# Choosing the most loaded expert two attention units earlier, and fetching its weights three units earlier

## The chip, the cores and the metric

The kernel runs on one core of a Trainium2 chip. The metric is device time in microseconds of one execution. The engines are TensorE (PE), VectorE (DVE), ScalarE (ACT), GpSimd (POOL) and SyncE (SP); SP computes nothing here and issues most DMA transfers, in program order, while POOL issues the indirect ones.

## The reference

Three stages follow one another on 1536 tokens of width 512:

```python
# attention: 2 batches, 8 heads, 768 positions, 64 wide
scores_l = scale * q @ k.T, kept where abs(i - j) < 16      # local window
scores_s = scale * q @ k_sum.T + log(32)                    # 24 block summaries: max of k, mean of v
x = softmax([scores_l, scores_s]) @ [v, v_sum]              # 1536 x 512
# mixture of 8 experts: tokens with x @ w_skip > 0 take their best expert, the others pass
e = argmax(xc @ w_gate); gate = softmax(xc @ w_gate)[e]
out[do] = xc + gate * (relu(xc @ w1[e]) @ w2[e])            # w1: 512 x 1024, w2: 1024 x 512 per expert
# feed-forward, 512 -> 2048 -> 512, with a piecewise quadratic g
out = g(x @ w_in) @ w_out
```

## The kernel before

Attention is cut into 24 **units**; unit i handles one 128-token tile and half of the heads, so that tile t is finished by units 2t and 2t+1 (the first six units go through their three tiles twice). Two units share a pair of V blocks. The units are software-pipelined: in the loop step of unit i, PE transposes the probabilities of unit i+1 (`stage_t`, tile `pt`), makes the scores of unit i+3 (`stage_s`, tile `s`), multiplies unit i's probabilities by V (`stage_pv`, tile `xo`), and between them prepares the q and k of the second batch (`prep`, tiles `tpk` and `pb`, up to unit 9). The order of the program in this stage is written by hand: `at(i, f, ...)` appends a function to the list of unit i, and the list is emitted behind unit i's `stage_pv`, in the order of the `at` calls. Every engine runs its own instructions in that order.

V is loaded by `load_v(b, j)` in blocks of 64 tokens, j = 0 to 11 for each batch, into six buffers `vw` that are used in turn. In the text **V1.j** is block j of the second batch; for j below 6 a small load from `vs_d` with the block summaries follows it (`put_vs`). Unit 12 reads V1.0 and V1.1, unit 14 reads V1.2 and V1.3, unit 16 reads V1.4 and V1.5, unit 18 reads V1.6 and V1.7, and so on. A buffer becomes free when the units that read its old block are done, so V1.2 and V1.3 wait for unit 9, V1.4 and V1.5 for unit 11, V1.6 and V1.7 for unit 13.

While attention runs, the tokens of finished tiles are routed: `r1` and `r2` make their expert scores, `r3` the one-hot choice and the running counts `run[t]` (a chain of small DVE instructions), `r4` each token's place, and POOL scatters the place lists and the rows to DRAM. Two experts' weights are wanted during attention already. The first is **the most loaded expert among the first three tiles**: `top` lets PE sum the counts (`count(3)`, a matmul with `run[3]`, tile `cnt`), and nine DVE instructions make an index of it in `placei`; `top_reg` loads that index into an SP register. `fetch(0, c)` for c = 0 to 3 then brings that expert's weights, 1 MB each, into the four `b8` buffers (in the text **W0 to W3**; line 129), and `split_hi` on ACT and `split_lo` on DVE (line 145) cut them into a high and a low part from unit 15 on, a half megabyte per unit. After attention, expert 0 is applied to its block of 128 tokens, then the other experts and the feed-forward follow.

All loads named here, V blocks and fetches alike, go through SP's one queue; a load that waits on SP holds back those behind it.

Of the kernel before, what the change touches and what calls it, by code (L numbers as in the profile page):

```python
# [40 lines left out]
def tile_net(ctx, tc, q, k, v, w_skip, w_gate, w1, w2, w_in, w_out, out):  # L41
# [243 lines left out]
    def attention(actx):  # L285
# [444 lines left out]
        def at(i, f, *a):  # L730
            todo[i].append(lambda: f(*a))
# [28 lines left out]
            at(c + 2, store_vs, c)  # L760
        rest = [(1, n // 4, n % 4) for n in range(16)]

        at(10, top)
        at(11, top_reg)
        at(16, early)
        at(17, early_places)
        at(18, early_regs)
# [3 lines left out]
        at(21, fetch, 1, 1)  # L771
        at(22, fetch, 1, 2)
        for c in range(4):
            at(12 + c, fetch, 0, c)

        pieces = [(0, c, i) for c in range(4) for i in range(4)]
        for n, x in enumerate(pieces):
# [544 lines left out]
    with ExitStack() as actx:  # L1322
        with tc.manual_schedule():
            attention(actx)
# [38 lines left out]
```

## Time and profile before

| | us |
|---|---|
| median of 3 runs | 550.04 |
| lowest, highest | 548.15, 554.98 |
| profiled execution, its own time | 547.05 |
| span in that profile, first to last instruction | 545.3 |

The profiled execution is one run of the same program, 3 us under the median of the others, and 1.75 us of it lie outside the span. PE is busy for 91% of the span, DVE for 65%, ACT for 52%. The page cuts the span into 40 slices of 13.6 us; attention fills about the first ten.

### The profile page before, as it was taken

To read this page: it belongs to the slowest core of one execution; us is meant where nothing else is said; L and a number is where in the kernel's file an instruction comes from. 1 tells how busy PE (TensorE), PEld (TensorE's weight loads), DVE (VectorE), ACT (ScalarE), POOL (GpSimd) and SP (SyncE) were. 2 spreads that over 40 slices of the span, in tenths; PEclk is the share of its full clock that TensorE was granted. 3 is DMA by queue.
4 is the path that set the end of the run, shared out by engine and by line. 5 is a ranking of instruction groups with operands and counts; after the bars stand their busy time and mean duration, and the time that the engine had idled before them with its cause. 6 is when DMAs were issued, how large, how long until landed. Compare 5 with 4: busy or idle time off the path is not lost.

```text
span 545.3 us, 7782 instructions
## 1 busy us (share of the span) xinstructions
PE 494.0 (91%) x2742; PEld 402.5 (74%) x2742; DVE 355.5 (65%) x714; ACT 285.7 (52%) x512; POOL 108.5 (20%) x159
## 2 busy tenths in 40 slices
PE   7777979688989999986899999999999999999990
PEld 4666868577678888854678887888888888888880
DVE  6667776769688978899999998443334443333340
ACT  6475545653457777682587776542334333333330
POOL 8406431503534131332000000020000020000002
PEclk8999999875989999998899999999999999999996
DMA  8997417996289887897435646020000011000002
GB/s 197 220 221 174 99 38 196 231 242 195 69 302 360 278 291 274 298 362 267 143 120 190 230 164 209 22 78 0 1 0 1 0 40 39 1 1 1 0 1 82
DMA packets 66761, 76.84 MB, mean 141 GB/s; under 512 B 31046, under 2 KB 48486, under 8 KB 66328
## 3 DMA queue, kind: packets, MB, share of 16 engines
q1 hardware_dynamic: 63256, 67.99, 43.1%
q0 software_dynamic: 3456, 8.26, 4.6%
q8 instruction: 23, 0.38, 0.3%
q14 instruction: 26, 0.21, 0.2%
HBM read 69.55 MB, written 8.12 MB: 142 GB/s over the span
## 4 chain that ended last, share of the span: by engine, by line
PE 38%; issue 33%; DVE 11%; DMA 7%; ACT 5%; POOL 2%; SPq 1%; POOLq 0%; ACTq 0%; DVEq 0%
PE hf L1146 7%; PE hp L935 5%; PE yp L959 5%; DMA vw<-in_v_dram 3%; PE s L437 3%; PE tph L945 2%; PE o L1187 2%; PE o L1185 2%; PE o L1186 2%; DVE w L145 2%; POOL out_dram L1197 1%; PE lp L492 1%; PE xo L466 1%; ACT p L442 1%; DMA raw<-in_q_dram 1%
## 5 line engine op out<-in xcount | busy, mean ns | idle before, releaser
L1146 PE MATMUL hf<-xh,w 128*128 128x512 f32 x384 | 128.2, 397 | 1.2 <-ACT xh L257 0.7
L1146 PEld LDWEIGHTS hf<-xh,w 128*128 128x128 f32 x384 | 72.5, 190 | 17.8 <-ACT w L1111 1.0
L145 DVE TENSOR_TENSOR w<-stg,w 128x1024 fp32r<-128x1024 f32 (+1 forms) x72 | 76.5, 1097 | 6.8 <-ACT w L139 6.8
L1185 PE MATMUL o<-w,g 128*128 128x512 f32 x192 | 77.1, 401 | 2.2 <-ACT g L1171 2.2
L1186 PE MATMUL o<-w,g 128*128 128x512 f32 x192 | 76.6, 399 | 0.0
L1146 PE MATMUL hf<-xl,w 128*128 128x512 f32 x192 | 75.5, 393 | 0.0
L1187 PE MATMUL o<-w,g 128*128 128x512 f32 x192 | 71.3, 399 | 0.0
L139 ACT CAST w<-stg 128x1024 fp32r<-128x1024 f32 (+1 forms) x72 | 65.0, 958 | 2.9 <-PE yp L280 1.5
L1156 ACT ACTIVATE c<-c,scal 128x512 f32<-128x512 f32 x32 | 23.2, 724 | 76.7 <-DVE c L1155 76.6
L1197 POOL DMA_INDIRECT out_dram<-ob,perm x12 | 11.8, 982 | 255.2 <-DVE ob L1196 165.0
L1166 DVE TENSOR_TENSOR hf<-hf,c 128x512 f32<-128x512 f32 x48 | 33.5, 698 | 39.5 <-ACT hf L1164 37.7
L1155 DVE TENSOR_SCALAR c<-hf 128x512 f32<-128x512 f32 x32 | 22.1, 692 | 42.3 <-PE hf L1146 42.3
L1172 DVE TENSOR_TENSOR g<-hf,g 128x512 fp32r<-128x512 f32 x48 | 33.1, 689 | 22.7 <-ACT g L1171 22.6
L1185 PEld LDWEIGHTS o<-w,g 128*128 128x128 f32 x192 | 36.5, 190 | 10.8 <-ACT g L1171 2.7
L442 ACT ACTIVATE p<-s,nm 128x120 f32<-128x120 f32 x96 | 26.7, 361 | 31.3 <-DVE nm L439 23.7
L1187 PEld LDWEIGHTS o<-w,g 128*128 128x128 f32 x192 | 36.6, 191 | 8.7
L1171 ACT CAST g<-hf 128x512 fp32r<-128x512 f32 x48 | 28.1, 585 | 28.4 <-DVE hf L1166 28.2
L1146 PEld LDWEIGHTS hf<-xl,w 128*128 128x128 f32 x192 | 36.3, 189 | 8.8 <-DVE xl L258 0.7
L1186 PEld LDWEIGHTS o<-w,g 128*128 128x128 f32 x192 | 36.6, 190 | 8.3
L224 POOL DMA_INDIRECT xf<-x,ids x10 | 24.5, 2455 | 64.4 <-DVE x L967 63.2
L959 PE MATMUL yp<-w,hT 128*128 128x512 f32 x128 | 34.6, 407 | 2.3 <-DVE w L145 2.2
L935 PE MATMUL hp<-w,xT 128*128 128x512 f32 x128 | 34.3, 416 | 2.1 <-DVE xT L924 1.3
(211 smaller groups left out, 825.4 us busy)
## 6 DMA issues: line engine op xcount, KB each, us to landing
stg<-in_moe_w_dram SPq DMA_DIRECT2D x32, 1024.0 KB, 6.7
raw<-in_moe_w_in_dram SPq DMA_DIRECT2D x14, 512.0 KB, 3.8
raw<-in_moe_w_out_dram SPq DMA_DIRECT2D x14, 512.0 KB
vw<-in_v_dram SPq DMA_DIRECT2D x20, 192.0 KB, 5.8
x<-xf SPq DMA_DIRECT2D x12, 264.0 KB, 6.6
raw<-in_k_dram SPq DMA_DIRECT2D x16, 192.0 KB, 4.3
raw<-in_q_dram SPq DMA_DIRECT2D x16, 192.0 KB, 4.1
vraw<-in_v_dram SPq DMA_DIRECT2D x4, 768.0 KB, 9.2
```

Source lines behind the costliest of these rows:

```text
L139: copy(out=part(wset[p, c // 2][0], c % 2, i, pieces), in_=part(stage[p, c], 0, i, pieces))
L145: eng.tensor_tensor(out=lo, in0=part(stage[p, c], 0, i, pieces), in1=hi.bitcast(F32), op=ALU.subtract)
L442: nc.scalar.activation(out=p[:, u], in_=s[:, u], func=AF.Exp, bias=nm[:, u:u + 1], scale=1.0)
L935: nc.tensor.matmul(hp, xT[:, kk], w[:, kk, 512 * f:512 * f + 512], start=(kk == 0 and w is hi), stop=(kk == 3 and w is lo))
L959: nc.tensor.matmul(yp, hT[:, kk], w[:, kk], start=(kk == 0 and w is hi), stop=(kk == 7 and w is lo))
L1146: nc.tensor.matmul(hp, w[:, 128 * kk:128 * kk + 128], a[:, kk], start=(n == 0), stop=(n == 11))
L1166: nc.vector.tensor_tensor(out=hp, in0=hp, in1=c, op=ALU.add)
L1171: nc.scalar.copy(out=gh, in_=hp)
L1172: nc.vector.tensor_tensor(out=gl, in0=hp, in1=gh.bitcast(F32), op=ALU.subtract)
L1185: nc.tensor.matmul(ops[ch][t], gh[:, a], hi, start=(f == 0), stop=False)
L1186: nc.tensor.matmul(ops[ch][t], gh[:, a], lo, start=False, stop=False)
L1187: nc.tensor.matmul(ops[ch][t], gl[:, a], hi, start=False, stop=(f == NF - 1))
```

## The change

`top` moves from the list of unit 10 to that of unit 8, where it stands directly behind the `r3` that makes its input `run[3]`; `top_reg` moves from unit 11 to 9, and the four fetches from units 12 to 15 to units 9 to 12. What is computed, and which expert is chosen, stays as it was.

```diff
-        at(10, top)
-        at(11, top_reg)
+        at(8, top)
+        at(9, top_reg)
         at(16, early)
...
         for c in range(4):
-            at(12 + c, fetch, 0, c)
+            at(9 + c, fetch, 0, c)
```

On SP this changes the order of the second batch's loads. In the following rows `vw_133` and `vw_134` are the buffers of V1.2 and V1.3; the place is just behind the load of V1.1.

```order
+L644 TENSOR_LOAD placei
+L644 ISA x2
+L129 ISA
+L129 DMA stg<-in_moe_w_dram 128x2x1024
 L385 DMA vw_133<-in_v_dram 96x8x64
 L376 DMA vw_133<-vs_d 24x8x66
+L129 ISA
+L129 DMA stg<-in_moe_w_dram 128x2x1024
 L385 DMA vw_134<-in_v_dram 96x8x64
 L376 DMA vw_134<-vs_d 24x8x66
```

The register load and W0 now stand ahead of V1.2, and W1 ahead of V1.3; W2 follows ahead of V1.4 and W3 ahead of V1.5. Before, the register load stood behind V1.3, W0 ahead of V1.5, W1 ahead of V1.6, W2 ahead of V1.7 and W3 behind it. The instructions behind V1.10 are the same.

On PE the count moves to the end of unit 8 (`tpx` is the transpose of `r1`, `pt` the first matmul of unit 9's step):

```order
 L466 MATMUL xo<-vw_134,pts 64x66 x2
 L482 MATMUL tpx<-ident,x_73 128x128 x4
+L600 LDWEIGHTS ones
+L600 MATMUL cnt<-runs,ones 128x8
 L449 MATMUL pt<-ident,p 120x128 x4
 L397 MATMUL tpk<-ident,raw 128x128 x3
```

It stood at the same place two units later, between `tpx` and `pt` at the end of unit 10.

On DVE the nine instructions of `top` come directly behind the last one of `r3`, ahead of unit 9's first:

```order
 L530 TENSOR_SCALAR se<-se 128x3
+L602 TENSOR_TENSOR cnt_1002<-cnt,eoff 1x8
+L653 TENSOR_SCALAR key<-cnt_1002 1x8
+L654 TENSOR_TENSOR key<-key,idx 1x8
+L583 TENSOR_TENSOR cmpt<-key 1x64
+L587 TENSOR_REDUCE rank<-cmpt 1x8
+L611 TENSOR_SCALAR top<-rank 1x8
+L617 TENSOR_TENSOR m<-idx,top 1x8
+L619 TENSOR_REDUCE top_1015<-m 1x1
+L622 CAST placei<-top_1015 1x1
 L404 TENSOR_SCALAR pb_130<-tpk 64x12x32
```

They stood behind the last instruction of unit 10's `stage_pv`. ACT's and POOL's instructions keep their order.

## Rows read from the trace of the kernel before

**Rows 1.** The page: span, and PE's granted clock in 40 slices.

```profile
span 545.3 us, 7782 instructions
...
PEclk8999999875989999998899999999999999999996
```

**Rows 2.** Waits of PE, 60 to 160 us: who waited for what, total, times, longest.

```profile
PE xo L466 <- DMA vw<-in_v_dram: 5.3, 1, 5.3
PE xo L466 <- DMA vw<-vs_d: 2.3, 1, 2.3
...
PE lp L492 <- ACT xs L483: 0.4, 1, 0.4
```

**Rows 3.** The chain that ended last, 88 to 152 us: start, us, what.

```profile
94.57 16.31 DMA vw<-in_v_dram
...
149.40 2.35 DMA x<-xf,ids
```

**Rows 4.** Timeline of PE: start, us, instruction, count, idle before it and its releaser.

```profile
66.28 0.66 PE L482 MATMUL tpx<-ident,x 128*128 128x128 f32 x4
...
69.99 0.55 PE L397 MATMUL tpk<-ident,raw 128*128 128x128 f32 x3 [1.20 <-ACT xs L483]
...
88.08 0.74 PE L466 MATMUL xo<-vw,pts 120*64 120x66 f32 x16
...
97.36 0.65 PE L466 MATMUL xo<-vw,pts 120*64 120x66 f32 x12 [2.34 <-DMA vw<-vs_d]
...
110.93 1.14 PE L466 MATMUL xo<-vw,pts 120*64 120x66 f32 x12 [5.34 <-DMA vw<-in_v_dram]
```

**Rows 5.** Timeline of SP's issues: V1.3, W0, V1.5, V1.7.

```profile
72.15 0.32 SPq L385 DMA_DIRECT2D vw<-in_v_dram  x1
...
82.29 2.22 SPq L129 DMA_DIRECT2D stg<-in_moe_w_dram  x1
84.61 0.41 SPq L385 DMA_DIRECT2D vw<-in_v_dram  x1
...
94.57 1.33 SPq L385 DMA_DIRECT2D vw<-in_v_dram  x1
```

**Rows 6.** Tile views: issue to landing of V1.3, W0 and V1.7.

```profile
DMA to landing us min/median/max: 3.3/3.3/3.3
...
DMA to landing us min/median/max: 12.7/12.7/12.7
...
DMA to landing us min/median/max: 16.3/16.3/16.3
```

**Rows 7.** Timeline of DVE: end of unit 8's routing, and the choice in unit 10.

```profile
70.11 0.56 DVE L523 TENSOR_TENSOR runs<-runs,ohb 128x8 bf16<-128x8 bf16 x3
...
71.06 0.56 DVE L404 TENSOR_SCALAR pb<-tpk 64x384 f32<-64x384 f32 x1
...
78.43 0.14 DVE L602 TENSOR_TENSOR cnt<-cnt,eoff 1x8 f32<-1x8 f32 x1
...
80.06 0.14 DVE L622 CAST placei<-top 1x1 int32<-1x1 f32 x1
```

**Rows 8.** Waits of DVE, 94 to 139 us, the two largest.

```profile
DVE den L469 <- PE xo L466: 4.9, 2, 4.6
DVE nm L439 <- PE s L437: 1.8, 2, 1.6
```

**Rows 9.** Windows: stretch, length, engines' busy us, PE clock, DMA share, GB/s.

```profile
76.00:80.00 4.00, 3.63 (x50) 3.28 (x44) 3.62 (x24) 2.08 (x6) 2.61 (x3) 1.00 0.01 0
...
82.00:88.00 6.00, 6.00 (x72) 5.59 (x70) 2.96 (x9) 4.22 (x12) 1.96 (x2) 1.00 0.46 66
88.00:92.00 4.00, 3.99 (x56) 3.52 (x55) 2.73 (x14) 2.30 (x7) 0.00 (x0) 1.00 0.97 378
92.00:98.00 6.00, 3.65 (x41) 3.33 (x40) 5.35 (x35) 2.91 (x9) 2.32 (x3) 1.00 1.12 246
98.00:104.00 6.00, 5.98 (x51) 5.54 (x51) 5.47 (x28) 3.58 (x10) 4.54 (x5) 0.72 1.23 254
```

## The prediction

> **What bounds the kernel now.** I read the page first, for where the clock falls: PE is granted nearly full speed everywhere but in slices 8 to 10, about 95 to 136 us [rows 1]. That is the second half of attention, so something starves PE there. The waits of PE over that stage name it: two waits of `xo`, unit 16's and unit 18's product with V, for V blocks, 2.3 and 5.3 us, 7.7 together; beside these PE hardly waits between unit 10 and unit 18 (one wait of 0.4 us is listed in it) [rows 2]. The timeline puts the two at 95.0 to 97.36 and 105.6 to 110.93 [rows 4]. The chain that ended last says whether they matter: one of its pieces is a single V transfer, from its issue at 94.57 to 110.88, 16.31 us long [rows 3]. So at unit 18 the program waits for V1.7 and nothing else. Third, SP's issues say why a V block of 0.2 MB needs so long. V1.3, issued at 72.15 with nothing ahead of it, landed in 3.3 us; W0, issued at 82.29, took 12.7; V1.5 was issued behind W0, and V1.7 behind W2, and that one took 16.3 [rows 5, 6]. The V blocks queue behind the fetches. Last, the windows show room that isn't used: from 76 to 80 us no byte moves, while 88 to 92 runs at 378 GB/s and 92 to 104 at about 250 [rows 9]. The fetches are started at the end of a pause and then stand in front of the V blocks.
>
> DVE shows how much of PE's 7.7 us counts. From 94 to 139 us its two largest waits are 4.9 us for `xo` (4.6 at unit 18, so 0.3 at unit 16) and 1.8 us for the scores that a restarted PE made late [rows 8]. So the wait at unit 16 is nearly free, DVE being full there (5.35 of 6 us [rows 9]), and the most that perfect V blocks can give back is 4.9 + 1.8 = 6.7 us.
>
> **Part 1, the choice moves to unit 8.** The count needs `run[3]`, which DVE writes until 70.11 + 0.56 = 70.67 [rows 7]. PE reaches the new place of the count at 66.28 + 0.66 = 66.94 [rows 4] and now has to stand there for 3.7 us; before, it ran on and waited 1.2 us a little later [rows 4]. Queued behind the count on PE are unit 9's transposes and scores, which ACT and DVE want. On DVE the nine instructions took from 78.43 to 80.20, 1.77 us [rows 7]; they now stand between the end of `r3` and the copy at 71.06 [rows 7], which is on the way to unit 10's scores. So unit 10 comes 1.8 us later. In unit 10 the same 1.77 us go away, but PE lost at most 0.4 us there [rows 2], so little comes back: I take +1.5 us for the units from 10 on. The bounds are 0 (DVE is full again from unit 14 on, and in its own queue the work has only moved) and 3.2: with PE idle for 3.7 us its clock may fall as it did after the 2.3 us wait, when it had 0.72 of full speed for 6 us, 0.28 x 6 = 1.7 us of lost work [rows 9].
>
> **Part 2, the fetches go ahead of V1.2 to V1.5.** `placei` is written at 71.06 + 1.77 = 72.8 instead of 80.20 [rows 7]. W0 was issued 2.1 us after it [rows 5, 7], with V1.4 in between, so now at about 74.5, 8 us sooner. The buffers that the fetches take over are raw tiles of prepared units and block sums; V1.2 and V1.3, which were issued at about 72, now wait for the register load, and each stands behind a fetch. By the shapes, a fetch has 128 x 2 x 1024 x 4 bytes, 1.05 MB, and a V block with its summary 96 x 8 x 64 x 4 + 24 x 8 x 66 x 4 bytes, 0.25 MB.
>  First need: V1.3 for unit 14, which PE starts at 88.08 [rows 4], now 89.6. Ahead of it are W0, V1.2 and W1: with itself 2.6 MB from about 76 on. At 378 GB/s that ends at 83, at 250 at 86.5 [rows 9]. No wait, if nothing slows it. What can is the stretch from 82 to 88, 66 GB/s [rows 9], when POOL's scatters of the first three tiles are being written; these hang on `r4` in unit 9 and should come 1.8 us later, from about 84.
>  Second need: V1.5 for unit 16, which PE reached at 95.0 [rows 4], now 96.5. Until it lands, four fetches, four V blocks and three row scatters of 0.27 MB must move, 6.0 MB. From 76 to 84 2.0 to 3.0 MB go (250 to 378 GB/s), to 90 another 0.4 MB, and 2.6 to 3.6 MB are left, 7 us at the high rate and 14.5 at the low one: V1.5 lands between 97 and 104.5. In the middle, 3.1 MB at 310 GB/s, it is 100. I take 100: unit 16 resumes 2.6 us later than at 97.36.
>  Third need: V1.7 for unit 18. It has no fetch behind V1.5 any more and lands 0.4 MB later, at 101 to 102, while unit 18 comes at 105.6 + 2.6. This wait of 5.3 us is gone.
>
> What the rule of the Trainium skill would make of this stands here by itself. DMA: Bandwidth & Descriptors, section "Queues, rings and completion order", says that on each DMA engine descriptors are consumed in ring order and that a transfer's completion lands only after earlier writes of that engine, across its queues. It speaks against the change: V1.2 to V1.5 can't overtake W0 to W3, nor be reported before POOL's writes. The trace agrees that V blocks come in behind the fetches issued ahead of them (3.3 us alone, 16.3 us behind W2 [rows 6]). The sum above moves no block ahead of a fetch; the rule's full weight is the slower rival below, 554 us.
>
> **The sum.** DVE worked without a pause to speak of from 94 until its wait of 4.6 us at unit 18, which ended just after 112. It is therefore free at 107.5, now 2.6 us later, at 110.1, and finds V1.7 there: 4.6 - 2.6 = 2.0 us sooner than before. PE doesn't have to restart, so the wait of 1.6 us for scores right behind it [rows 8] goes too: 2.0 + 1.6 = 3.6 us. The rest of the chain to 151.75 is DVE's routing, POOL's scatters and small transfers, the last of them the gather at 149.40 [rows 3]; none of that waits for a fetch of expert 0, and the fetches of the next expert are released by DVE's splits, so all of it should come 3.6 us sooner, and what follows with it. What is late next is DVE itself, and behind it the same chain. W0 to W3 landing sooner gives nothing of its own: `split_hi` starts in unit 15 as before. 547.05 - 3.6 = 543.45 for the profiled execution; that one lies 3.0 us under the median of the runs, and on the median it is 550.04 - 3.6 = **546.4 us**. With V1.5 at 97, part 1's 1.5 us sets the delay: 4.6 - 1.5 + 1.8 = 4.9 us of gain; with V1.5 at 102 the gain is 1.6. Forecast alone: 545 to 548.5.
>
> **The rivals.**
>  (A) The wait only moves. W1 isn't through when POOL's slow stretch begins (the 2.0 MB case), V1.3 lands at some 93, and PE waits 3 us in unit 14 on top of part 1's 1.5. Then DVE is at unit 16 at 98 + 4.2 and at unit 18 at 111.7: 0.4 us gained there, and half of the 1.6 behind it. About 1 us, **549 us**. For it: the 66 GB/s of that stretch. Against it: from 76 to 80 nothing else moves.
>  (B) Slower: the four fetches in a row hold V1.5 until 104.5, the low end of the rates. PE resumes unit 16 7.1 us later than before, DVE reaches unit 18 at 107.5 + 7.1 = 114.6 instead of 112.1, +2.5; PE has stood for 8 us, so the clock costs its 1.7 us, and the wait for scores stays: +4.2, **554 us**. It decides from V1.5 landing at 97.36 + 4.6 = 102 on. For it: V1.7 needed 16.3 us behind W2, and V1.5, issued at about 87 and behind W3, would be at 103.5 with that. Against it: W0 and most of W1 go in the pause.
>  (C) More gain: the fetches keep 378 GB/s, V1.5 is there at 96.5, and part 1's delay is taken up by DVE's fuller queue: both waits of DVE go, 6.7 us, **543.3 us**. For it: DVE waits only 0.3 us at unit 16 now. Against it: 250 GB/s over 92 to 104.
>  That the change doesn't do what it says is excluded as far as the order goes; the index is ready when SP asks for it, since SP waits for it.
>
> **How the numbers follow.** Forecast 0.55, A 0.20, B 0.14, C 0.11. The predicted time is the forecast's, 546.4. The range leaves out most of B and the far half of C, and the runs before lie 6.8 us apart from lowest to highest: 541.5 to 551.5. A difference of under 2%, 11 us, is about what a measurement of this kernel can't tell from none; all four cases lie inside it, and only B with a wait at unit 14 on top comes near it: faster 0.02, same 0.95, slower 0.03.
>
> **What would show it.** In the profile after: PE idle for 3 to 4 us before the count, near 70; W0 issued near 74.5 and bytes moving from 76 to 80; no wait of `xo` at unit 14; one of 2 to 5 us at unit 16; none at unit 18; DVE's wait for `xo` in that stage down from 4.9 to 1 or 2 us; and the gather before the first pair of small experts landing near 148 instead of 151.75. If PE waits at unit 14, A was right; if unit 16 resumes behind 102, B; if DVE waits elsewhere for as long, the DVE-bound reading is wrong. The time would also be missed if the stages behind 152 us take back the gain, for instance by a clock that falls at another place.

## The result, and the profile after

The changed kernel takes 552.11 us (median of 20 runs), the kernel before 548.67 (20 runs). The ratio is 1.0066, with a 95% interval of 1.0043 to 1.0089: some 3.6 us slower (3.4 by the medians), where 3.6 us less were forecast. It is under the 2% that this measurement calls a change, but the interval excludes a gain.

The page of the changed kernel, its span and PE's granted clock in 40 slices:

```profile
span 555.1 us, 7782 instructions
...
PEclk9898788979689999999899999999999999999996
```

This execution (556.79 us) is a slow one among the runs of its kernel, as the profiled one of e10 (556.00 us) is further down. Its first dip of the clock, in slice 5, lies ahead of the change. So the rows below are from a second profiled execution of the changed kernel (run e1, span 551.4). In both, PE stands 3.8 us before the count and waits for no V block. The waits of PE in e1, from 60 to 160 us, answer to [rows 2]:

```profile
PE cnt L600 <- DVE runs L523: 3.8, 1, 3.8
...
PE xo L466 <- remote: 2.8, 1, 2.8
```

No wait for a V block is among them, at no unit. There is the announced one for `runs`, and a wait of an `xo` that names no transfer; "remote" means that the trace shows no event of this core that released it. PE's timeline around the count answers to [rows 4]:

```profile
67.63 0.66 PE L482 MATMUL tpx<-ident,x 128*128 128x128 f32 x4
72.07 0.17 PE L600 MATMUL cnt<-runs,ones 128*128 128x8 bf16 x1 [3.78 <-DVE runs L523]
72.09 1.09 PE L449 MATMUL pt<-ident,p 128*120 128x128 f32 x4
...
74.02 1.90 PE L437 MATMUL s<-pb 128*128 128x120 f32 x8
...
89.26 0.95 PE L466 MATMUL xo<-vw,pts 120*64 120x66 f32 x16 [2.81 <-remote]
```

DVE's timeline of unit 9, answering to [rows 7]: end of the routing, first and last instruction of the choice, and the three instructions behind it.

```profile
72.21 0.17 DVE L530 TENSOR_SCALAR se<-se 128x3 f32<-128x3 f32 x1
72.28 0.15 DVE L602 TENSOR_TENSOR cnt<-cnt,eoff 1x8 f32<-1x8 f32 x1
...
73.90 0.14 DVE L622 CAST placei<-top 1x1 int32<-1x1 f32 x1
74.40 0.56 DVE L404 TENSOR_SCALAR pb<-tpk 64x384 f32<-64x384 f32 x1 [0.36 <-ACT pb L407]
75.95 0.66 DVE L439 TENSOR_REDUCE nm<-s 128x4 f32<-128x480 f32 x1 [1.00 <-PE s L437]
78.38 0.56 DVE L404 TENSOR_SCALAR pb<-tpk 64x384 f32<-64x384 f32 x1 [1.77 <-ACT pb L407]
```

The choice takes 72.28 to 74.04, 1.76 us, as forecast. Behind it stands a wait that wasn't in the sum: 1.00 us for scores, which PE made in 1.90 us at half clock. SP's issues of W0, V1.2 and W1, and the windows (columns as in [rows 9]), show that the fetches did go out in the pause:

```profile
75.15 0.43 SPq L129 DMA_DIRECT2D stg<-in_moe_w_dram  x1
77.25 0.32 SPq L385 DMA_DIRECT2D vw<-in_v_dram  x1
...
78.37 0.41 SPq L129 DMA_DIRECT2D stg<-in_moe_w_dram  x1
```

```profile
72.00:76.00 4.00, 3.93 (x19) 3.80 (x19) 2.33 (x15) 1.09 (x2) 0.00 (x0) 0.50 0.00 0
76.00:80.00 4.00, 4.00 (x48) 3.46 (x48) 2.10 (x7) 2.21 (x6) 0.00 (x0) 0.92 0.94 297
```

From 76 to 80 us 297 GB/s move where none did before. The traffic did what the change wants of it; the time didn't follow.

### The profile page after: what moved, and what is told of

It reads as the page before. It is cut to its first block, busy times and chain, and to the rows that moved or that the text cites. A ratio compares the mean times of both kernels' runs of the same rounds, so it can differ in the third digit from the quotient of the medians.

```text
span 555.1 us, 7782 instructions
## 1 busy us (share of the span) xinstructions
PE 502.4 (91%) x2742; PEld 409.6 (74%) x2742; DVE 355.8 (64%) x714; ACT 286.3 (52%) x512; POOL 108.2 (19%) x159
## 4 chain that ended last, share of the span: by engine, by line
PE 41%; issue 34%; DVE 13%; ACT 6%; DMA 2%; POOL 2%; SPq 0%; another core or an unknown queue 0%; POOLq 0%; ACTq 0%; DVEq 0%
PE hf L1146 7%; PE hp L935 5%; PE yp L959 5%; PE s L437 3%; DVE w L145 3%; PE tph L945 2%; PE o L1187 2%; PE o L1185 2%; PE o L1186 2%; PE yp L280 2%; PE xo L466 2%; PE hp L264 1%; POOL out_dram L1197 1%; PE tpk L397 1%; DVE nm L439 1%
## 5 line engine op out<-in xcount | busy, mean ns | idle before, releaser
L1166 DVE TENSOR_TENSOR hf<-hf,c 128x512 f32<-128x512 f32 x48 | 33.5, 698 | 39.5 <-ACT hf L1164 36.4
```

Source lines behind the costliest of these rows:

```text
L1166: nc.vector.tensor_tensor(out=hp, in0=hp, in1=c, op=ALU.add)
```

## The experiments

Three questions went through them. First whether the moved choice (P) or the moved traffic (D) costs the time; then whether POOL's list writes (its indirect writes of place lists) stop the program in most executions of either kernel (F), or the changed order does (C); last how list writes and V waits hang together. One table carries the comparison. It cuts each profiled execution at DVE's first instruction behind the V product (L469) of a unit, so a unit's length is the distance of two such starts; all in us.

| kernel | unit 8 to 9 | 9 to 10 | 10 to 11 | 10 to 18 | 18 to end | ratio to before (95%) |
|---|---|---|---|---|---|---|
| before | 6.6 | 3.0 | 3.0 | 34.4 | 433.2 | |
| e5 before again | 6.6 | 3.0 | 7.7 | 39.0 | 430.7 | 1.0015 (0.9978 to 1.0052) |
| e6 before, third | 6.6 | 3.0 | 7.6 | 38.7 | 429.8 | one run |
| after | 9.1 | 3.0 | 4.8 | 39.5 | 430.7 | 1.0066 (1.0043 to 1.0089) |
| e1 after again | 9.5 | 3.0 | 6.3 | 38.6 | 430.7 | 1.0046 (1.0007 to 1.0085) |
| e2 choice alone | 9.5 | 3.0 | 7.8 | 39.2 | 430.8 | 1.0012 (0.9979 to 1.0045) |
| e3 fetch one unit sooner | 6.6 | 3.0 | 7.8 | 39.4 | 432.9 | 1.0037 (0.9992 to 1.0082) |
| e4 choice in unit 9 | 6.6 | 4.7 | 6.1 | 39.0 | 430.2 | 1.0028 (0.9983 to 1.0072) |
| e7 before, 3 list writes out | 6.6 | 3.0 | 3.8 | 33.9 | 430.6 | 0.9908 (0.9865 to 0.9951) |
| e8 before, 7 out | 6.6 | 3.0 | 3.9 | 30.0 | 430.8 | 0.9795 (0.9746 to 0.9845) |
| e9 after, 7 out | 9.5 | 3.0 | 3.9 | 29.2 | 430.5 | 0.9852 (0.9802 to 0.9901) |
| e10 rows first | 6.6 | 3.0 | 6.7 | 40.2 | 436.6 | 1.0013 (0.9973 to 1.0054) |
| e11 rows first, one group | 6.6 | 3.0 | 8.2 | 41.2 | 429.9 | 1.0000 (0.9960 to 1.0040) |
| e12 first lists held | 6.6 | 3.0 | 4.0 | 37.0 | 431.0 | 0.9938 (0.9907 to 0.9969) |
| e13 after, stand filled | 8.3 | 3.0 | 7.0 | 39.3 | 431.2 | 1.0005 (0.9966 to 1.0045) |
| e14 after, first lists held | 9.5 | 3.0 | 3.9 | 39.2 | 430.3 | 1.0055 (1.0023 to 1.0087) |

The column of unit 8 to 9 splits cleanly by where the choice stands. That of 10 to 18, where the forecast looked for its gain, doesn't split by the change among the kernels that write their lists as the kernel before does: there the first profile of before, on which the forecast was built, is the odd one out.

**e1, the changed kernel again.** No edit.

> The changed kernel once more, for a second profile. Its first profile shows no wait of PE for V blocks any more, PE idle 3.8 us before the count of unit 8, and two stretches (85 to 97 us and 109 to 121 us) in which DVE, ACT and PE wait for updates of PE's semaphore that come up to 3 us after the matmul. Theory P (the moved choice costs): the idle before the count and 1.8 us of DVE chain come again, the two stretches were an accident of that execution, and the time is 2 to 4 us over the kernel before. Theory D (the moved traffic costs): a stretch of 3 us or more in which all engines wait comes again beside POOL's first row scatters.

The slowdown came again, 1.0046, with an interval that just excludes no change. Signs of both theories came: for P the stand and a longer unit 8 to 9, for D a stretch in unit 10 to 11 in which DVE waits 4.5 us, ACT 4.7 and PE 2.8. So e1 alone doesn't decide.

**e2, the choice alone.** The fetches stay at units 12 to 15.

```diff
+        at(8, top)
+        at(9, top_reg)
...
             at(12 + c, fetch, 0, c)
```

> The choice in unit 8 and its register load in unit 9, the fetches left in units 12 to 15. Theory P: the whole cost is here, 2 to 5 us slower than the kernel before, PE idle 3 to 4 us before the count, and the two V waits still there (2.3 and 5.3 us, the first shorter by the delay). Theory D: within 1.5 us of the kernel before, since the traffic keeps its place.

**e3, the fetches one unit sooner**, as early as the old choice allows.

```diff
         at(10, top)
         at(11, top_reg)
...
+            at(11 + c, fetch, 0, c)
```

> The choice left in units 10 and 11, the fetches one unit sooner, in units 11 to 14, the soonest that the old choice allows. Theory P: V1.7 no longer stands behind W2 directly, so its wait of 5.3 us shrinks to 0 to 4 us and the time is 1 to 4 us lower than before. Theory D: the fetches meet the row scatters as before or worse; no gain, 0 to 2 us slower.

**e4, the choice one unit sooner**, in unit 9, the fetches from 10 on.

```diff
+        at(9, top)
+        at(10, top_reg)
...
+            at(10 + c, fetch, 0, c)
```

> The choice in unit 9 instead of 10 or 8, its register load and the first fetch in unit 10, the fetches in units 10 to 13. The counts that the choice needs are then a unit old, so PE should not stand before the count. Theory P: no idle before the count over 0.5 us, V waits gone or under 2 us in total, and 2 to 4 us faster than before. Theory D: the traffic is nearly that of the changed kernel, so 1 to 4 us slower than before, with all engines waiting beside the first row scatters.

The gains that P expected of e3 and e4 didn't come, nor did the V waits that it expected in e2. The ratios of these three lie between no change and that of e1, and their intervals can't split 3 us between the parts. The traces can: e2 has the longer unit 9 (9.5) and e3 hasn't (6.6), while both take 39 us from unit 10 to 18. e4 has no wait ahead of the count; there the nine instructions cost 4.7 - 3.0 = 1.7 us, their bare length. Alone of these kernels (e1 to e4) it shows V waits, 0.8 us in unit 14 and 2.3 us in unit 16:

```profile
PE xo L466 <- DMA vw<-in_v_dram: 3.0, 2, 2.3
```

**e5 and e6, the kernel before again**, to see what its other executions look like. No edit.

> The kernel before once more, for a second profile. In the five profiles of the changed kernel and its variants PE's semaphore updates come up to 7 us late in two stretches, 2 to 3 us behind the start of POOL's list scatters (units 10 to 12 and 16 to 17); in the one profile of the kernel before they never come late in attention. Theory F (a freeze that belongs to the scatters and happens in most executions of either kernel): the late updates come here too, unit 10 to 11 takes 6 us or more instead of 3.0, unit 16 to 17 8 us or more instead of 5.3, and the wait of 5.3 us for V1.7 is gone or under 2 us, because the freeze gives the V blocks time; the span is 549 to 553 us. Theory C (the changed order causes it): no late updates, unit 10 to 11 about 3 us, the V waits of 2.3 and 5.3 us again, span 544 to 547 us.

> The kernel before a third time. Theory F: as in the second profile, late updates in both stretches and no V wait over 2 us. Theory C: as in the first profile.

Neither shows a V wait. The waits of PE (60 to 160 us) and of DVE (60 to 139) in e5, against [rows 2] and [rows 8]:

```profile
PE xo L466 <- remote: 4.1, 1, 4.1
```

```profile
DVE nm L439 <- PE s L437: 5.1, 4, 2.9
DVE den L469 <- remote: 4.6, 1, 4.6
```

e6 has the same 4.1 and 4.6. The timelines of POOL, PE, DVE and ACT in e5 show the stop at unit 11:

```profile
75.94 1.08 POOL L556 DMA_INDIRECT ids_d<-slot,si  x1 [8.12 <-DVE x L567]
...
78.62 0.98 POOL L556 DMA_INDIRECT ids_d<-slot,si  x1 [0.30 <-issue]
79.90 0.98 POOL L224 DMA_INDIRECT xf<-x,slot  x1 [0.30 <-issue]
```

```profile
77.56 0.74 PE L466 MATMUL xo<-vw,pts 120*64 120x66 f32 x16
...
79.59 0.63 PE L449 MATMUL pt<-ident,p 128*120 128x128 f32 x4
...
80.26 1.05 PE L437 MATMUL s<-pb 128*128 128x120 f32 x8
85.44 0.84 PE L466 MATMUL xo<-vw,pts 120*64 120x66 f32 x16 [4.13 <-remote]
```

```profile
84.50 0.16 DVE L469 TENSOR_SCALAR den<-xo 128x4 f32<-128x4 f32 x1 [4.57 <-remote]
```

```profile
84.71 0.59 ACT L451 COPY pts<-pt 120x512 f32<-120x512 f32 x1 [3.57 <-remote]
```

PE finished `xo` at 78.3 and `pt` at 80.2. The readers of both, DVE and ACT, went on at 84.5 and 84.7 only, and PE then lacked what they make. All three engines stood, while POOL wrote lists and rows. A second stop follows the next group of lists (99.37): unit 16 to 17 takes 9.4 us, 5.3 in the first profile of before. F held for the stops: they are in kernels with either order. Its time didn't: it expected a span of 549 to 553 us, and e5 has 546.5 and e6 544.8, against 545.3 in the first profile. Units 10 to 18 are 4.3 to 4.6 us longer in e5 and e6, and what lies behind unit 18 is 2.5 to 3.4 us shorter; why is open. So of these three executions the one with V waits isn't the slower one, and which form the other runs had isn't known.

**e7, the kernel before without the list writes of tiles 0 to 2**; the place lists lack these tokens, so later stages work on other rows.

```diff
             for i, t in enumerate(ts):
+                if t < 3:
+                    continue
                 d = nc.gpsimd.indirect_dma_start(out=ids_d[:, :],
```

> The kernel before without the list scatters of the first three tiles (their places in the lists stay empty; the row scatters stay). Theory F with the list scatters as its cause: no late updates in units 10 to 12, unit 10 to 11 takes 3 to 4 us, the stretch at units 16 to 17 stays; 2 to 6 us faster than the kernel before. If the row scatters are the cause: the late updates in units 10 to 12 stay. Theory C: no difference of more than 1 us.

The first stop is gone (3.8 us), the second stays (unit 16 to 17: 9.3 us), and the ten runs are 5 us faster than the kernel before, as F expected. The gain isn't made by the tokens that the lists lack: behind unit 18 e7 and e8 take 430.6 and 430.8 us, e5 430.7. The windows of 80 to 88 us tell what became of the traffic; first e5's, then e7's:

```profile
80.00:84.00 4.00, 1.30 (x11) 1.09 (x9) 0.00 (x0) 1.12 (x4) 2.84 (x3) 1.00 0.54 83
84.00:88.00 4.00, 2.56 (x25) 2.41 (x26) 2.17 (x8) 2.29 (x6) 0.00 (x0) 0.75 0.55 51
```

```profile
80.00:84.00 4.00, 4.00 (x46) 3.77 (x45) 2.26 (x8) 2.47 (x9) 0.00 (x0) 1.00 0.83 201
84.00:88.00 4.00, 4.00 (x46) 3.68 (x44) 1.54 (x5) 2.63 (x7) 0.00 (x0) 1.00 1.07 328
```

83 and 51 GB/s with the three small writes, 201 and 328 without them, with the same row writes. It is the counterpart of the slow stretch that the prediction read in [rows 9] (66 GB/s). SP's issue of V1.7, which waits for unit 13, shows that the writes delay the V blocks in the first profile's form too. There it is at 94.57 [rows 5]; in e7, at 86.70, though unit 13 starts alike (85.63 there, 85.54 in e7):

```profile
86.70 0.85 SPq L385 DMA_DIRECT2D vw<-in_v_dram  x1
```

The slow traffic isn't what stops the engines, though. In the changed kernel (e1) DVE stands for 4.5 us up to 88.33, and in that time 312 GB/s move; the slow stretch follows:

```profile
88.33 0.16 DVE L469 TENSOR_SCALAR den<-xo 128x4 f32<-128x4 f32 x1 [4.48 <-remote]
```

```profile
84.00:88.00 4.00, 2.45 (x21) 2.24 (x21) 0.00 (x0) 1.27 (x5) 3.08 (x4) 1.00 1.31 312
88.00:92.00 4.00, 2.74 (x25) 2.63 (x26) 2.25 (x8) 1.81 (x6) 0.59 (x1) 0.78 1.12 93
```

**e8 and e9, both kernels without the list writes of tiles 0 to 6**, the same edit with `t < 7`.

> The kernel before, with the place lists of tiles 0 to 6 left out (seven small indirect writes, three of them in unit 9 and four in units 15 and 16), so that the lists hold no token of these tiles and the output is not the reference's. With its pair, the changed kernel with the same writes left out, it asks whether the forecast's gain exists when the two freezes don't take the place of the waits for V. Theory W (the V waits bind as soon as the freezes are gone, as the profile of before was read): PE waits some 2 us at unit 16 and some 5 us at unit 18 for V blocks, units 10 to 18 take about 34 us, and the time is 5 to 10 us under the kernel before. Theory N (the V waits were of one execution only): no wait for V over 1 us, units 10 to 18 take 29 to 31 us, 8 to 10 us under the kernel before.

> The changed kernel, with the place lists of tiles 0 to 6 left out (output not the reference's). Theory W: no V wait at unit 18 and one of at most 3 us at unit 16, units 10 to 18 shorter than in its pair by 3 to 5 us, the earlier choice costs its 3 us, and the two come out within 2 us of each other, this one 0 to 2 us ahead. Theory N: no V wait in either, units 10 to 18 alike, and this one 3 us behind its pair.

Theory N held, with more gained (11 us) than its 8 to 10. In e8's waits of PE (60 to 140 us) the largest is no longer a transfer, and e9's has only the stand for `runs` on top:

```profile
PE cnt L602 <- ACT p L442: 1.6, 1, 1.6
```

```profile
PE cnt L602 <- DVE runs L523: 3.8, 1, 3.8
```

Units 10 to 18 take 30.0 and 29.2 us, so V blocks and fetches have room in either order, and the sooner fetches give 0.8 us at most. The ratios of the pair lie 0.57% apart, some 3 us, and by their intervals alone the two can't be told apart. In the traces unit 8 to 9 loses 9.5 - 6.6 = 2.9 us and units 10 to 18 give back 0.8.

**e10, row writes ahead of list writes**, and **e11, the list writes of tiles 0 to 2 emitted in unit 15.** `r4l` holds `r4`'s loop of list writes; first e10's edit, then e11's:

```diff
                 at(i + 4 - (t == 6), r5, of[t])
+                at(i + 4 - (t == 6), r4l, of[t])
```

```diff
+                if t == 5:
+                    at(i + 4, r4l, of[0])
```

> The kernel before, with POOL's row writes of every group of tiles issued ahead of its list writes instead of behind them. Theory L (the small list writes make the freeze, whatever stands ahead): the freeze in which PE's updates come late moves behind the row writes, 2 to 5 us later, and lasts as long; units 10 to 18 again take about 39 us, the time is within 0.4% of the kernel before. Theory S (the first indirect writes after a pause make it, whatever they write): the freeze stays where it was, 2 to 3 us after POOL starts, and the list writes behind the rows cost nothing; the time is again the same, since only the place tells them apart. If the row writes keep POOL so busy that the list writes spread out, up to 3 us may be gained.

> The kernel before, with the list writes of tiles 0 to 2 held back to unit 15, where they are issued with those of tiles 3 to 5; what is computed stays as it was. Theory L: one freeze is gone, units 10 to 11 take 3 to 4 us instead of 7.7, and the time is 3 to 5 us under the kernel before, unless six list writes in a row double the second freeze, then it is the same. If V waits of 2 to 5 us at units 16 and 18 come up in place of the freeze, the gain is 0 to 2 us.

e11 didn't do what was meant: POOL runs ahead of the other engines, and with nothing to wait for it issued the lists at once, behind the rows. POOL's timeline in e11:

```profile
75.77 1.08 POOL L224 DMA_INDIRECT xf<-x,slot  x1 [8.51 <-DVE x L559]
...
79.74 0.98 POOL L566 DMA_INDIRECT ids_d<-slot,si  x1 [0.30 <-issue]
```

So both are tests of rows first, and neither L nor S came out: the lists start 3.8 us later in e11 than in e5, yet DVE's stop ends at 84.46 there and at 84.50 in e5, where L wanted it later; and rows alone make none (e7, e8), against S. Lists are needed for the stop, but their start doesn't set its end. The times can't be told from that of before (1.0013 and 1.0000, 0.4% either way).

**e12, the first lists really held.** DVE copies their places in unit 15, and POOL's writes read that copy:

```diff
+        def held():
+            si1 = per.tile([128, 3], I32, name="si1")
+            nc.vector.tensor_copy(out=si1, in_=rs.pop('held'))
+            lists(of[0], si1)
...
+                    at(i + 4, held)
```

> The kernel before, with the list writes of tiles 0 to 2 really held back: a copy of their places, made by DVE at the start of unit 15's list, is what POOL's list writes read, so that POOL issues them together with those of tiles 3 to 5, at about 97 us in place of 76; the row writes of tiles 0 to 2 stay where they were. What is computed stays as it was. Theory B (each burst of list writes makes one freeze of about the same length, however many writes are in it): unit 10 to 11 takes 3 to 4 us in place of 7.7, unit 16 to 18 stays at 13 to 14, and the time is 3 to 5 us under the kernel before, a ratio of about 0.992. Theory Q (the freeze is the traffic that the writes make, so much for each write): the first freeze is gone, the second is twice as long, 9 us in place of 4.4, and the time is that of the kernel before within 2 us; or above it, if the list load of the first block of expert 0 in unit 18 now waits for the writes.

POOL's timeline and the windows of 80 to 88 and 98 to 104 us:

```profile
93.12 0.98 POOL L535 DMA_INDIRECT ids_d<-slot,si  x1 [13.71 <-DVE sl L556]
...
99.57 0.98 POOL L535 DMA_INDIRECT ids_d<-slot,si  x1 [0.30 <-issue]
```

```profile
80.00:84.00 4.00, 4.00 (x46) 3.77 (x46) 2.28 (x9) 3.00 (x10) 0.00 (x0) 1.00 0.78 217
84.00:88.00 4.00, 4.00 (x51) 3.68 (x50) 1.62 (x6) 2.38 (x7) 0.00 (x0) 1.00 1.10 322
...
98.00:104.00 6.00, 2.65 (x12) 2.18 (x12) 2.05 (x13) 0.04 (x1) 4.50 (x5) 0.50 0.75 117
```

The first stop is gone (4.0 us), with 217 and 322 GB/s in its place; the second grew, units 15 to 18 taking 21.3 us against 18.5 in e5. Between B and Q, then: 3.7 us spared in unit 10 to 11, 2.8 paid back in units 15 to 18. At 0.9938 it is some 3.4 us faster than the kernel before, which is under 2%, but the interval excludes no change.

**e13, the stand filled**: 16 products of zeros ahead of the count, read by nobody.

```diff
         def top():
+            busy(16)
             ra = sort8(keyed(count(3)), False)
```

> The changed kernel with 16 products of zeros on PE ahead of the count, some 3.4 us of work that fills the stand for run[3]; their result is read by nobody. Theory K (the clock behind the stand is what makes the scores late): PE stays at full clock, the eight score products after the count take 1.05 us in place of 1.5 to 1.9, DVE's wait of 0.6 to 1.0 us for them goes, unit 8 to 9 takes 8.4 to 8.6 us, and the time is 1 us under the changed kernel, a ratio of 1.002 to 1.004 to the kernel before. Theory T (the stand itself makes them late): the products take less time, but unit 8 to 9 still takes 9.1 to 9.5 us.

PE's timeline:

```profile
64.92 3.40 PE L789 MATMUL busy<-zb 128*128 128x480 bf16 x16
68.86 0.17 PE L600 MATMUL cnt<-runs,ones 128*128 128x8 bf16 x1 [0.54 <-DVE runs L523]
...
69.89 1.05 PE L437 MATMUL s<-pb 128*128 128x120 f32 x8
```

The clock behind the count is 1.00 in e13; the same stretch was granted 0.50 in e1 (above), and 0.50 in e7 too, where PE had no such stand:

```profile
68.00:72.00 4.00, 3.46 (x43) 2.94 (x42) 3.49 (x19) 1.08 (x3) 0.00 (x0) 1.00 0.00 0
```

```profile
72.00:76.00 4.00, 3.95 (x27) 3.29 (x26) 2.97 (x20) 1.32 (x3) 0.11 (x1) 0.50 0.31 67
```

Theory K held: the scores take 1.05 us again, and unit 8 to 9 takes 8.3 us, a little under its 8.4 to 8.6. What is left over 6.6 is 1.7 us, the length of the nine instructions. The time is that of before within 0.5% (1.0005), so the 1 us that K expected is not shown by the runs. In e7 the half clock cost nothing (unit 9 to 10 takes 3.0 us); it costs where scores are waited for.

**e14, the changed kernel with e12's edit.**

> The changed kernel with the list writes of tiles 0 to 2 held back as in e12 (held till unit 15; output as the reference's). Theory C (the change costs the earlier choice, and its sooner fetches are worth nothing): unit 8 to 9 takes 9.1 to 9.5 us, units 10 to 18 take 37 us as in e12, and the time is 3 us behind e12's ratio of 0.9938, that is about 0.999 of the kernel before. Theory G (the sooner fetches pay once the first jam is gone, for all the blocks of V are in before the second): units 10 to 18 take 34 to 35 us, and the time equals e12's, about 0.994.

G fell: units 10 to 18 take 39.2 us, not less than e12's 37.0, and the ratio is 1.0055. C was right about unit 9 (9.5) but not on the rest: the one stop behind the six lists grew by another 2.9 us (units 15 to 18: 24.2), and the time is 1.2% behind e12's ratio, not 0.5%. So with the lists held the change costs more than the earlier choice: units 10 to 18 take 2.2 us more as well. Why the stop is longer with the fetches issued sooner is open.

## Why the prediction was wrong

**The step that failed** is the first one: that "at unit 18 the program waits for V1.7 and nothing else", and that perfect V blocks "can give back" up to 6.7 us. It was read rightly from [rows 2 to 4, 8], but these rows are of one execution, and two further profiled ones of the same kernel have no V wait. There the program stops for 4.7 us (7.7 - 3.0) in unit 10 to 11 and about 4 us in unit 16 to 17, PE, DVE and ACT together, and the V blocks are in when they are asked for. (That the stops give them the time is argued: these traces don't show when they land.) So the two terms of the gain, 2.0 and 1.6 us, had nothing to be taken from: units 10 to 18 take 38.7 and 39.0 us before (e6, e5) and 39.5 and 38.6 after. The prediction had named the sign of this: "if DVE waits elsewhere for as long, the DVE-bound reading is wrong". In e1 DVE waits 4.5 us in unit 10 to 11, in e5 4.6. Whether the change gains in an execution that has V waits and no stops isn't known, since none of the changed kernel's traces is of that form.

**What stands behind both forms** is, as far as shown, POOL's list writes. The prediction noted the stretch of 66 GB/s of [rows 9] and put it down to POOL's scatters, as a delay to its fetches. The runs show which scatters and what they weigh: without the list writes of tiles 0 to 2 the same stretch moves 201 to 328 GB/s and 5 us are gained (e7), without seven of them 11 us (e8), and neither stops nor V waits are left, with the order of V blocks and fetches as it was. That the V waits of the first profile come of these writes too is borne out by V1.7, issued 7.9 us sooner in e7 without three of them; but each form rests on one to three profiled executions, and what chooses between them isn't known. The order can cost a wait too: e4 waits 0.8 and 2.3 us in units 14 and 16.

**Part 1** had the right pieces and too small a sum. PE's stand of 3.7 us measured 3.78, the nine instructions 1.77 measured 1.76, W0's issue at 74.5 came at 75.15, in an execution that was 1.4 us later at unit 8. I took 1.5 us of bounds 0 to 3.2; unit 8 to 9 grew by 2.5 to 2.9 us, and unit 10, from whose list the choice went away, gave nothing back that can be seen (10 to 11: 3.9 in e8 and in e9, the pair without stops). The upper bound named the rest: 1.2 us (9.5 - 8.3, e13) go when the stand is filled and PE keeps its clock, which was granted at 0.50 from 72 to 76 behind the stand. That it would count I had left out of the value taken.

**Part 2** moved the bytes from 76 to 80 as described, and was worth nothing: with stops (e2 against after) or without (e8, e9) units 10 to 18 are alike within 1 us, and with the first lists held they are 2.2 us longer (e14 against e12). The wait of 2 to 5 us in unit 16 that it announced didn't come. That there is none at unit 18 came true, but not by the change: e5 and e6 have none there either. What is left is part 1's cost, some 3 us, which is near the measured 3.6 (2.4 to 4.9 by the interval). The runs don't show that split: the ratio of e13 is 0.3 us over before, with an interval up to 2.5 us, and that of e2 0.6 us, up to 2.5 us, which is under the 2.9 that its own trace loses in unit 8 to 9. So the split by parts rests on the traces.

**The rivals.** B's time (554) and A's (549) lie on either side of the result, but neither mechanism occurred in the changed kernel, since no V block was late in unit 14 or 16. B's sign, unit 16 behind 102, did come (its DVE step starts at 106.3 in e1), but behind the stop in unit 10 to 11. The last sign, the gather that was to land near 148 in place of 151.75 [rows 3], is in the chain of the changed kernel's first profile:

```profile
160.13 2.27 DMA x<-xf,ids
```

It landed at 162.40, 10.7 us later, of which 4.7 us were there at unit 8 already (72.75 against 68.08).

## What to carry to other kernels

A wait of a few microseconds in one profiled execution is a candidate, not a bound: profile the unchanged kernel a second time before taking a gain from it, and look for what the waits of several executions have in common, here POOL's list writes ahead of them. Moving a consumer to directly behind its producer makes an in-order engine stand; price the stand with everything queued behind it and with the clock that follows, and fill it or place it one step later (e4: 1.7 us, no stand); neither made this kernel faster than before. To hold small indirect writes back, give them a true data dependency: their engine ran ahead of a later place in the program (e11) and kept to the dependency (e12). What that is worth depends on the rest: some 3.4 us in the kernel before, nothing in the changed one (e14).

## What the runs showed of the hardware

Three list writes, 128 values of 4 bytes each, cost about 5 us of the whole program (e7), though POOL spends 1 us on issuing each. Behind their start DVE and ACT stood for some 4 us (4.57 and 3.57 in e5) and went on 4.5 to 6.2 us after the trace has the products that they read ended. Transfers ran at 51 to 83 GB/s meanwhile in e5, at 312 in e1. How a list write holds these engines up, and why in the first profile of before V blocks came late instead, stays open: the stop's end isn't set by when the lists start (e11), and its length isn't fixed for each write (e12). Behind a stand of 3.78 us PE was granted half its clock for the next products (eight score products 1.90 us in place of 1.05), and with the stand filled it wasn't (e13); in e7 it was granted half at that place without such a stand.
